# One x slab by plain load, two more by DMA transposes of their own, and W1's first slab in halves: the start of a one-core gated mix kernel

## The chip, the cores and the metric

The program runs on one core of a Trainium2 chip. The metric is device time of one execution in microseconds (us). Quoted times are medians over the runs of a kernel, and a ratio is the mean time of one kernel's runs over that of the other's runs of the same rounds on the same chip, so it is not quite the ratio of the quoted medians. A profile is one single execution; its span is about 1.3 us shorter than the time of that run.

Words used below: a *slab* is one of five 128-row pieces of the contraction dimension (D = 640), of W1 or of x. PE is the matmul engine, SP the engine that issues most DMAs, ACT and DVE the two elementwise engines. "Landing" is the moment the last of a DMA's 16 completion counts arrives.

## The reference, cut to what matters

```python
x = A_x                                        # [1, 2048, 640], bf16
g = sigmoid((x * gate_w).sum(-1))
a = ssm(x)                                     # B projection, complex scan, C projection, skip
b = gelu(x @ w1 + b1) @ w2 + b2                # w1 [640, 1728], w2 [1728, 640]
return g * a + (1 - g) * b
```

The kernel works in four quarters of 512 rows of x. Its first real work is `x @ w1` for quarter 0 and the first 1024 columns of w1: eight output tiles, five slabs each, 40 steps of 128x128 by 512 columns. This is called the first W1 group.

## The kernel before: the parts that matter

The tensor engine needs x transposed (contraction on partitions). x's slabs 0 and 1 of quarter 0 come by a plain load and are transposed on PE, with a copy from PSUM by DVE; slabs 2, and 3 with 4, come by DMA transposes. SP issues these loads one after the other, in this order:

```python
KN = 2
load("xna", "sp", ..., xn[0][:, :, 0:KN * 128], x2[0:512, 0:KN * 128]...)   # x slabs 0, 1
w1load(0, "sp", 1)                       # W1 slab 0, 256 KB
w1load(1, "sp", 1.3)
xtrans(0, range(KN, KN + 1), 1.6, 0.8)   # x slab 2, DMA transpose
w1load(2, "sp", 2)
xtrans(0, range(KN + 1, KD), 3, 1.3)     # x slabs 3 and 4, one DMA transpose
w1load(3, "sp", 4)
w1load(4, "sp", 5)
# ... then the rest of W1, the transposes of B, more of x, W2, C
```

PE runs warm-up matmuls on a constant until x arrives, then the transposes, then the first W1 group slab by slab:

```python
def f_warm():
    for n in (512,) * 6 + (256,):
        nc.tensor.matmul(PS[4][:, 0:n], one..., one..., start=True, stop=True)

for i, (k, c0, c1) in enumerate(((0, 0, 2), (0, 2, 4), (1, 0, 2), (1, 2, 4))):
    # two 128x128 transposes on PE, then a copy by DVE into xT[0][:, k, ...]
# ... (cut)
steps = [(0, 0, 0), (0, 1, 0), (0, 0, 1), (0, 1, 1)] + [(k, jf, None) for k, jf in seq if k or jf > 1]
# each step waits for its W1 slab and its x slab; slab-major order, 8 PSUM banks
```

Tile 7 of slab 0 is put off until just before tile 7 of slab 1, because its bank is used for the transposes. So PE needs slab 1 after seven steps, and 33 steps are then still to come; 24 from slab 2 on, 16 from slab 3 on, 8 from slab 4 on.

## Time and profile before

| | before |
|---|---|
| median on record at the prediction | 213.72 us (3 runs) |
| median, 6 runs beside the change | 213.16 us (212.76 to 213.74) |
| span of the profile | 211.5 us (its run took 212.76) |
| first W1 matmul | 4.57 us |
| end of the first W1 group | 13.27 us |

The profile page's chain that ended last, of the kernel before:

```profile
PE 98%; issue 0%; DVE 0%
```

The wait view for PE, same kernel (engine, line, what it waited for: us in total, times, longest):

```profile
PE ps L400 <- PEq L968: 0.8, 1, 0.8
PE ps L685 <- issue: 0.2, 1, 0.2
```

PE is the bottleneck and, in this view, waits only 0.2 us once it has begun. The timeline of PE, same kernel, cut at 3 us so that only the last three warm-up matmuls show (start us, length us, engine, line, what, count):

```profile
2.44 1.27 PE L400 MATMUL ps<-const-bfloat16-1.0 128*128 128x512 bf16 x3
3.67 1.06 PE L412 MATMUL ps<-ident,xn 128*128 128x128 bf16 x8
4.57 2.54 PE L622 MATMUL ps<-xT,W1sb 128*128 128x256 bf16 x13
6.95 0.22 PE L431 MATMUL ps<-ident,rows 128*128 128x128 bf16 x1
7.01 6.42 PE L622 MATMUL ps<-xT,W1sb 128*128 128x512 bf16 x28
13.27 1.03 PE L642 MATMUL ps<-xT,W1sb 128*128 128x512 bf16 x4
```

Start to start, a warm-up matmul of 512 columns takes 0.427 us and a W1 matmul of 512 columns 0.2157 us: PE is at half rate until about 4.5 us. (The row of the page that shows the granted clock is full throughout; it does not show this half rate.)

The timeline of SP, same kernel (start us is the moment of issue, the second number how long SP was busy issuing):

```profile
0.74 0.45 SPq L326 DMA_DIRECT2D xn<-in_A_x_dram  x1
1.25 0.96 SPq L326 DMA_DIRECT2D W1sb<-in_B_w_dram  x2
2.26 1.20 SPq L333 DMA_TRANSPOSE xT<-in_A_x_dram  x1
3.51 0.59 SPq L326 DMA_DIRECT2D W1sb<-in_B_w_dram  x1
4.15 1.28 SPq L333 DMA_TRANSPOSE xT<-in_A_x_dram  x1
5.47 2.10 SPq L326 DMA_DIRECT2D W1sb<-in_B_w_dram  x4
```

A transpose costs SP 1.20 us for one slab and 1.28 for two; a plain load 0.42 to 0.59. The DMA view of the first 7 us, same kernel (q1 is SP's queue, with packets, MB and the share of the 16 DMA engines' time that its packets took; in the lines of loads the last number is the median us from issue to landing):

```profile
DMA packets 2047, 1.30 MB, mean 186 GB/s; under 512 B 1151, under 2 KB 1663, under 8 KB 2047
...
q1 hardware_dynamic: 1959, 1.30, 69.6%
...
W1sb<-in_B_w_dram SPq DMA_DIRECT2D x5, 256.0 KB, 3.9
...
xT<-in_A_x_dram SPq DMA_TRANSPOSE x2, 4.1
```

### The profile page before, as it was taken

The page shows a single profiled execution, that of the slowest core. Times are in us where ns is not written, and L with a number is a line of the kernel's source. Part 1 is how long each engine was busy: PE and PEld are TensorE (multiplying, and loading weights), DVE is VectorE, ACT ScalarE, POOL GpSimd, SP SyncE. Part 2 cuts the span into 40 slices and gives each one's busy share as a digit, 9 for nine tenths or more (in the row PEclk, how much of TensorE's full clock was granted, in tenths as well). Part 3 has the DMA queues.
Part 4 walks back from the last instruction along what each step waited for, and adds up shares of the span by engine and source line. Part 5 has one row for each costly group of instructions (what it writes and reads, how often), then busy time and mean ns, then how long its engine had stood idle before and what let it go on. Part 6 is the DMA issues. An engine that isn't in the chain of part 4 may idle for free.

```text
span 211.5 us, 3140 instructions
## 1 busy us (share of the span) xinstructions
PE 208.1 (98%) x1266; PEld 121.2 (57%) x1276; DVE 189.3 (90%) x264; ACT 111.3 (53%) x201; POOL 3.0 (1%) x11
## 2 busy tenths in 40 slices
PE   8999999999999999999999999999999999999996
PEld 4444444444567776444466777544446777767775
DVE  2599999999999999999999969899999999899444
ACT  2588556678904334556953333456792444723330
POOL 2000000000000010000000001000000000000000
PEclk9999999999999999999999999999999999999999
DMA  5999699999100013100000014100000000010011
GB/s 164 290 246 183 158 225 300 303 213 197 42 0 3 31 38 120 62 0 0 0 3 0 0 48 143 39 23 3 0 0 2 3 31 31 31 34 0 31 34 62
DMA packets 31350, 16.35 MB, mean 77 GB/s; under 512 B 23144, under 2 KB 30440, under 8 KB 31336
## 3 DMA queue, kind: packets, MB, share of 16 engines
q1 hardware_dynamic: 30960, 14.83, 28.5%
q0 software_dynamic: 320, 1.31, 2.0%
q8 instruction: 10, 0.16, 0.3%
q14 instruction: 4, 0.03, 0.1%
q10 hardware_dynamic: 56, 0.01, 0.0%
HBM read 7.63 MB, written 2.62 MB: 48 GB/s over the span
## 4 chain that ended last, share of the span: by engine, by line
PE 98%; issue 0%; DVE 0%
PE ps L772 27%; PE ps L642 22%; PE ps L821 21%; PE ps L685 20%; PE ps L622 4%; PE ps L400 1%; PE ps L786 1%; PE ps L663 1%; PE ps L412 0%; DVE osb L855 0%; PE ps L431 0%
## 5 line engine op out<-in xcount | busy, mean ns | idle before, releaser
L772 PE MATMUL ps<-W2sb,Gl 128*128 128x320 bf16 x416 | 59.2, 299 | 0.0
L772 PEld LDWEIGHTS ps<-W2sb,Gl 128*128 128x128 bf16 x416 | 40.4, 98 | 17.1 <-issue 1.1
L642 PE MATMUL ps<-xT,W1sb 128*128 128x512 bf16 x215 | 47.5, 379 | 0.3
L821 PE MATMUL ps<-CT,H 128*128 128x320 bf16 (+2 forms) x330 | 45.5, 295 | 0.0
L725 DVE TENSOR_TENSOR_SCAN W<-atab,V 128x1280 bf16<-128x1280 f32 x16 | 44.3, 2811 | 0.3
L685 PE MATMUL ps<-xT,BT 128*128 128x512 bf16 x196 | 43.1, 379 | 0.3 <-issue 0.2
L821 PEld LDWEIGHTS ps<-CT,H 128*128 128x128 bf16 x330 | 31.9, 98 | 11.7
L800 ACT ACTIVATE E<-ps,g1col 128x320 bf16<-128x320 f32 x32 | 16.3, 526 | 39.7 <-PE ps L772 25.6
L642 PEld LDWEIGHTS ps<-xT,W1sb 128*128 128x128 bf16 x220 | 21.5, 98 | 26.0
L649 ACT ACTIVATE Gl<-ps,cols 128x512 bf16<-128x512 f32 x44 | 29.6, 688 | 10.0 <-PE ps L642 10.0
L685 PEld LDWEIGHTS ps<-xT,BT 128*128 128x128 bf16 x200 | 19.4, 98 | 23.5 <-ACT Gt L671 0.4
L694 ACT ACTIVATE U<-ps 128x512 bf16<-128x512 f32 x40 | 23.8, 597 | 15.0 <-PE ps L685 14.9
L832 ACT ACTIVATE E<-ps,gcol 128x320 bf16<-128x320 f32 x30 | 15.8, 527 | 22.6 <-PE ps L821 22.6
L759 ACT ACTIVATE ps<-b2b 128x320 f32<-128x320 bf16 x32 | 14.1, 441 | 1.1
L481 DVE TENSOR_TENSOR osb<-xg,E 128x640 bf16<-128x640 bf16 x15 | 7.3, 487 | 7.9 <-ACT E L832 7.6
L842 DVE SCALAR_TENSOR_TENSOR xg<-xn,gcol,dsk 128x640 bf16<-128x640 bf16 x16 | 13.9, 882 | 0.4
L597 DVE SCALAR_TENSOR_TENSOR scr<-xn,gwb 128x640 bf16<-128x640 bf16 x16 | 13.2, 822 | 0.4
L481 DVE TENSOR_TENSOR H<-H,V 128x1280 bf16<-128x1280 bf16 x16 | 12.5, 821 | 0.3
L481 DVE TENSOR_TENSOR V<-V,W 128x1280 bf16<-128x1280 bf16 x16 | 12.5, 821 | 0.3
L481 DVE TENSOR_TENSOR V<-mr,U 128x2560 bf16<-128x2560 bf16 x8 | 11.9, 1488 | 0.2
L481 DVE TENSOR_TENSOR H<-c,W 128x2560 bf16<-128x2560 bf16 x8 | 11.9, 1488 | 0.2
L481 DVE TENSOR_TENSOR W<-mi,U 128x2560 bf16<-128x2560 bf16 x8 | 11.9, 1483 | 0.0
(80 smaller groups left out, 99.9 us busy)
## 6 DMA issues: line engine op xcount, KB each, us to landing
out_dram<-osb SPq DMA_DIRECT2D x15, 160.0 KB, 1.8
W2sb<-in_B_w_dram SPq DMA_DIRECT2D x1, 2080.0 KB, 8.9
W1sb<-in_B_w_dram SPq DMA_DIRECT2D x5, 256.0 KB, 3.9
xn<-in_A_x_dram POOLq DMA_DIRECT2D x2, 640.0 KB, 4.6
xn<-in_A_x_dram SPq DMA_DIRECT2D x1, 640.0 KB, 7.9
W1sb<-in_B_w_dram SPq DMA_DIRECT2D x1, 480.0 KB, 5.8
W1sb<-in_B_w_dram SPq DMA_DIRECT2D x1, 400.0 KB, 6.5
xn<-in_A_x_dram SPq DMA_DIRECT2D x1, 384.0 KB, 6.0
```

Source lines behind the costliest of these rows:

```text
L481: return inc("dve", nc.vector.tensor_tensor(out=o, in0=a, in1=b, op=o_))
L642: t = nc.tensor.matmul(PS[bank][:, :], W1sb[:, k, jf * 128:(jf + 1) * 128], xT[q][:, k, :], start=(k == 0), stop=(k == KD - 1))
L649: return inc("act", nc.scalar.activation(Gl[q % 2][:, jf, :], PS[bank][:, :], ACT.Gelu_apprx_tanh, bias=b1col[:, jf:jf + 1]))
L685: t = nc.tensor.matmul(PS[bank][:, :], BT[:, ci, kd, k * 128:(k + 1) * 128], xT[q][:, kd, :], start=(kd == 0), stop=(kd == KD - 1))
L694: return inc("act", nc.scalar.activation(dst, src, ACT.Copy, scale=1.0 if ci == 0 else -1.0))
L725: t = inc("dve", nc.vector.tensor_tensor_scan(out=g[:, ci, :], data0=a, data1=v[:, ci, :], initial=0.0, op0=ALU.mult, op1=ALU.add))
L759: return inc("act", nc.scalar.activation(PS[bank][:, 0:HALF], b2b[:, cols], ACT.Copy))
L772: t = nc.tensor.matmul(PS[bank][:, 0:HALF], Gl[q % 2][:, jf, t4 * 128:(t4 + 1) * 128], W2sb[:, jf, cols], start=False, stop=False, skip_gr ...
L800: return inc("act", nc.scalar.activation(E1[c % NE][:, cols], PS[bank][:, 0:HALF], ACT.Copy, scale=g1col[:, c:c + 1]))
L821: t = nc.tensor.matmul(PS[bank][:, 0:n], H[b % NHB][:, ci, k, s * 128:(s + 1) * 128], CT[:, ci, k, cols], start=(i == 0), stop=(i == 2 * K ...
L832: return inc("act", nc.scalar.activation(E2[c % NE][:, cols], PS[bank][:, 0:HALF], ACT.Copy, scale=gcol[:, c:c + 1]))
L842: return inc("dve", nc.vector.scalar_tensor_tensor(out=xg[c % 2][:, :], in0=xn[q % 2][:, c % 4, :], scalar=gcol[:, c:c + 1], in1=dsk[:, :] ...
```

## The change

Its intent: start PE earlier. Only slab 0 of x comes by plain load, so that four PE transposes, two DVE copies and one warm-up matmul fall away. Slabs 1 and 2 each get a DMA transpose of their own, ahead of the W1 slab that goes with them. W1's slab 0 comes in halves, so that the first half is there sooner. A small filler matmul keeps PE busy while DVE copies. The diff, cut to its core:

```diff
-        KN = 2
+        KN = 1
         load("xna", "sp", ...)
-        w1load(0, "sp", 1)
+        for h in range(2):
+            f0, f1 = h * FW // 2, (h + 1) * FW // 2
+            load(f"w1_0{h}", "sp", f"l_w10{h}", W1sb[:, 0, f0:f1], B_w1[0:128, f0:f1], [("w1", 0, h)], prio=1 + 0.1 * h, lat=2.6)
+        xtrans(0, range(KN, KN + 1), 1.2, 0.8)
         w1load(1, "sp", 1.3)
-        xtrans(0, range(KN, KN + 1), 1.6, 0.8)
+        xtrans(0, range(KN + 1, KN + 2), 1.6, 0.8)
         w1load(2, "sp", 2)
-        xtrans(0, range(KN + 1, KD), 3, 1.3)
+        xtrans(0, range(KN + 2, KD), 3, 1.3)
         w1load(3, "sp", 4)
 ...
-            for n in (512,) * 6 + (256,):
+            for n in (512,) * 5 + (256,):
 ...
-        for i, (k, c0, c1) in enumerate(((0, 0, 2), (0, 2, 4), (1, 0, 2), (1, 2, 4))):
-            bank = (7, 6, 5, 7)[i]
+        for i, (k, c0, c1) in enumerate(((0, 0, 2), (0, 2, 4))):
+            bank = 7 - i
 ...
+        def f_fill():
+            return inc("pe", nc.tensor.matmul(PS[4][:, 0:192], one..., one..., start=True, stop=True))
+        op("fill", "pe", 0.2, (), [("bank", 4)], f_fill, prio=-980)
 ... (the waits of slab 0's matmuls go by half; cut)
```

More of the change, by code (lines that the diff above doesn't have):

```diff
@@ L413, in f_xt @@
                 return inc("pe", t)
-            op(f"xt{i}", "pe", 0.11 * (c1 - c0), ["xna", "ident"], [("bank", bank)], f_xt, prio=(-990, -989, -988, 2.5)[i])
+            op(f"xt{i}", "pe", 0.11 * (c1 - c0), ["xna", "ident"], [("bank", bank)], f_xt, prio=-990 + i)
             def f_xc(k=k, pt=pt, c0=c0, c1=c1):
@@ L420, in bass_gated_mix__ssm_conv_s5__dense_activation_gelu__prompt_kernel @@
             op(f"xc{i}", "dve", 0.42, [("bank", bank)], [("xT", 0, k, c0)], f_xc, prio=-2000 + i)
+        def f_fill():
+            return inc("pe", nc.tensor.matmul(PS[4][:, 0:192], one.broadcast_to([128, 128]), one.broadcast_to([128, 192]), start=True, stop=True))
+        op("fill", "pe", 0.2, (), [("bank", 4)], f_fill, prio=-980)
         XK0 = [[("xT", 0, k)] for k in range(KD)]
         XK0[0] = [("xT", 0, 0, 0), ("xT", 0, 0, 2)]
-        XK0[1] = [("xT", 0, 1, 0), ("xT", 0, 1, 2)]
         XT = {q: [("xT", q, k) for k in range(KD)] for q in range(1, NQ)}
@@ L623, in f_mm @@
                                                       start=(k == 0 and t0 == 0), stop=(k == KD - 1), skip_group_check=jf < 2))
-                op(f"m1_0_{jf}_{k}_{t0}", "pe", d_mm(t1 - t0), (XK0[k] if h is None else XK0[k][h:h + 1]) + [("w1", k)], [("bank", jf)],
+                op(f"m1_0_{jf}_{k}_{t0}", "pe", d_mm(t1 - t0), (XK0[k] if h is None else XK0[k][h:h + 1]) + ([("w1", k)] if k else [("w1", 0, jf // (NW // 2))]), [("bank", jf)],
                    f_mm, prio=pe_prio())
@@ L644, in f_mm @@
                     return inc("pe", t)
-                op(f"m1_{q}_{jf}", "pe", KD * d_mm(512), XT[q] + ([("w1", k) for k in range(KD)] if jf < NW else [("w1", "r", int(jf * 128 >= FM))]), [("bank", bank)], f_mm, prio=pe_prio())
+                op(f"m1_{q}_{jf}", "pe", KD * d_mm(512), XT[q] + ([("w1", k) for k in range(1, KD)] + [("w1", 0, 0), ("w1", 0, 1)] if jf < NW else [("w1", "r", int(jf * 128 >= FM))]), [("bank", bank)], f_mm, prio=pe_prio())
                 def f_ge(jf=jf, bank=bank):
```

## The prediction

> **What bounds it now.** The chain of waits is PE for 98% of the 211.5 us span; the wait view gives PE 0.8 us before its first matmul and 0.2 us elsewhere. The back-to-back part of the kernel cannot shrink by this change: it does the same matmuls. Only the start matters: when the first real matmul (W1 times x, quarter 0) begins, and whether slabs of W1 and x land fast enough for the 40 slab matmuls that follow.
>
> Timeline of before: 7 warm-up matmuls 0.78 to 3.5 (512 columns every 0.427 us); 8 PE transposes 3.67 to 4.57, the first released by the landing of x's 256 KB load (issued 0.74, landed 2.9 us later); first W1 matmul 4.57; from then 512 columns every 0.2155 us with no gap over 0.05 us until 13.27. So slab 1 is wanted at 6.09, slab 2 at 8.09, slab 3 at 9.81, slab 4 at 11.54. Landings (issue plus time to landing, DMA view): W1 slab 0 4.3, slab 1 5.7, x slab 2 6.3, W1 slab 2 7.2, x slabs 3-4 8.3, W1 slab 3 9.45, slab 4 10.2, first rest of W1 12.3 (wanted 13.27). Slab 3 has only 0.36 us to spare.
>
> **What the change saves.** One warm-up matmul (0.43), four PE transposes (4 x 0.107) and two copies leave; a 192-column filler (about 0.16) comes. The x load is halved in bytes, not in packets (512 of 256 B instead of 512 B; in the trace they take 18 against 27 ns): I estimate it lands 0.2 us earlier. Transposes at about 3.45, first copy 3.8 to 4.1 (0.29 us), first W1 matmul about 4.15 with the first half slab landed by then: 0.3 to 0.5 us gained, all on the critical path.
>
> **What it costs.** SP issues serially. A transpose costs it 1.20 us (one slab) or 1.28 (two), a plain load 0.42 to 0.59. The new queue has one more transpose ahead of W1's slab 1, so that slab is issued at 3.5 instead of 1.8, slab 2 at 5.5 instead of 3.5, slab 3 at about 7.4 instead of 5.5, slab 4 at 8.0 instead of 6.1. In before, loads land 3.0 to 4.1 us after issue. The queue ahead is shorter now, so I estimate about 3.1 to 3.5: slab 1 at 6.6 (wanted about 5.7), slab 2 at 8.5 to 8.9 (wanted 8.6 after the first stall), slab 3 at 10.6 to 11.0 (wanted 10.3), slab 4 in time. PE stalls of about 0.8 + 0.2 + 0.5 us replace the 0.4 gained. The first W1 group ends near 14.3 instead of 13.27. The rest shifts: the B transposes come about 1.2 us later, but have 1.5 us to spare.
>
> The Trainium skill, "TensorE: Matmul & The Clock Gate", Part 1, says half rate lasts until about 3.4 us of sustained activity, in a free-running window. This trace agrees: 0.427 us per 512 columns before, 0.2155 from 4.57. The new gaps are under 1 us, so I expect no long return to half rate; the switch may come a little late.
>
> **Prediction.** 213.72 - 0.4 + 1.1 = 214.4 us, range 213.2 to 215.5. Faster by over 2%: 0.01; within 2%: 0.97; slower by over 2%: 0.02.
>
> **What would show it.** First W1 matmul near 4.15 (right start); PE waits named after W1 or x landings before slab 1 and slab 3, about 0.5 us each or more (right cost); slab 1 issued at 3.5 and slab 3 at 7.4; everything after 20 us shifted rigidly by the same amount.
>
> **What would make it wrong.** Landing within 2.8 us of issue on the shorter queue: then the stalls nearly vanish and the result is 213.3 to 213.6. A clock switch one window late: up to 1.5 us more. The new order of DVE (gates against combines) making PE wait later on.

## The result, and the profile after

| | before | after |
|---|---|---|
| median of 6 runs | 213.16 us (212.76 to 213.74) | 214.34 us (214.09 to 214.83) |
| ratio | | 1.0055, 95% interval 1.0032 to 1.0077 |
| span of the profile | 211.5 us | 213.2 us (its run took 214.49) |
| first W1 matmul | 4.57 us | 3.94 us |
| end of the first W1 group | 13.27 us | 14.98 us |
| profile's end minus that | 198.2 us | 198.2 us |

The change is 0.55% slower, within the 2% that count as the same. PE starts its real work 0.63 us earlier and ends the first W1 group 1.71 us later; from there on both profiles take the same 198.2 us (211.5 - 13.27 and 213.2 - 14.98). So all of the loss is in the first 15 us. (Profile to profile it is 1.7 us, median to median 1.2: the profile of before fell on its fastest execution.)

The page's chain, of the changed kernel:

```profile
PE 94%; SPq 3%; DMA 2%; issue 0%; DVE 0%
```

The wait view for PE, changed kernel:

```profile
PE ps L629 <- DMA W1sb<-in_B_w_dram: 1.2, 2, 0.8
PE ps L403 <- PEq L975: 0.8, 1, 0.8
```

Two waits for W1 are new. The timeline of PE, changed kernel:

```profile
2.44 0.84 PE L403 MATMUL ps<-const-bfloat16-1.0 128*128 128x512 bf16 x2
3.13 0.61 PE L415 MATMUL ps<-ident,xn 128*128 128x128 bf16 x4
3.54 0.37 PE L426 MATMUL ps<-const-bfloat16-1.0 128*128 128x192 bf16 x1
3.94 2.38 PE L629 MATMUL ps<-xT,W1sb 128*128 128x256 bf16 x9
6.16 0.22 PE L438 MATMUL ps<-ident,rows 128*128 128x128 bf16 x1
6.83 3.94 PE L629 MATMUL ps<-xT,W1sb 128*128 128x512 bf16 x17 [0.45 <-DMA W1sb<-in_B_w_dram]
11.53 3.61 PE L629 MATMUL ps<-xT,W1sb 128*128 128x512 bf16 x16 [0.76 <-DMA W1sb<-in_B_w_dram]
```

From start to start of its matmuls, PE loses 0.62 us before slab 1, 0.11 before slab 2 and 0.93 before slab 3 (the view counts idle time only from the modelled end of the last matmul, so it says 0.45 and 0.76). And the nine matmuls of slab 0 take 2.2 us (3.94 to 6.16) instead of 1.5: in this execution the half rate lasts until about 5.4 us. PE is ready for slab 1 at 6.21 us, in before at 6.09: the whole head start of 0.63 us was gone before the first wait.

The timeline of SP, changed kernel, lines as above:

```profile
...
2.26 1.20 SPq L333 DMA_TRANSPOSE xT<-in_A_x_dram  x1
3.51 0.57 SPq L326 DMA_DIRECT2D W1sb<-in_B_w_dram  x1
4.13 1.13 SPq L333 DMA_TRANSPOSE xT<-in_A_x_dram  x1
5.31 0.58 SPq L326 DMA_DIRECT2D W1sb<-in_B_w_dram  x1
5.94 1.26 SPq L333 DMA_TRANSPOSE xT<-in_A_x_dram  x1
7.24 2.10 SPq L326 DMA_DIRECT2D W1sb<-in_B_w_dram  x4
```

Slab 1 of W1 is now issued at 3.51 (before: 1.79), slab 2 at 5.31 (3.51), slab 3 at 7.24 (5.47). The DMA view of the first 7 us, changed kernel:

```profile
DMA packets 2162, 0.98 MB, mean 140 GB/s; under 512 B 1752, under 2 KB 2008, under 8 KB 2162
...
q1 hardware_dynamic: 2074, 0.97, 68.3%
...
W1sb<-in_B_w_dram SPq DMA_DIRECT2D x2, 256.0 KB, 3.3
...
xT<-in_A_x_dram SPq DMA_TRANSPOSE x3, 3.1
```

Each transfer lands sooner after its issue (3.1 to 3.3 us instead of 3.9 to 4.1), yet fewer bytes have moved in the same 7 us: 0.98 MB instead of 1.30. That fits a queue that SP fills too slowly, but this view alone does not show it: the packets of SP's queue took almost the same share of the engines' time, 68.3% against 69.6%. Packets lasted longer, too: in the packet records of these 7 us, W1's 2 KB packets took 168 ns in the mean instead of 107 (median 84 in both). The count of bytes under the table of experiments tells more. The chain of waits in order of time, changed kernel (start us, us, what), shows what PE waited for in the end:

```profile
...
5.94 1.26 SPq L333
7.19 0.04 issue
7.24 4.16 DMA W1sb<-in_B_w_dram
11.40 0.14 issue
11.53 3.61 PE ps L629 x16
...
```

The chain no longer runs over PE in the first 11 us: it runs over SP's issues, from 0.74 us on, to W1's slab 3, which lands at 11.4 us.

A simple bound makes the profiles comparable: PE cannot end the first W1 group before a slab's landing plus its remaining steps at 0.2157 us. Landings here are issue plus time to landing, from the trace. For slab 3 this is 9.45 + 16 x 0.2157 = 12.90 in before (PE's own pace decides, 13.27) and 11.40 + 3.45 = 14.85 in the change (it ended at 14.98, with 0.14 us from landing to the first matmul).

### The profile page after: what moved, and what is told of

Its sections match the earlier page's. It is cut to its first block, busy times and chain, and to the rows that moved or that the text cites. A ratio compares the mean times of both kernels' runs of the same rounds, so it can differ in the third digit from the quotient of the medians.

```text
span 213.2 us, 3142 instructions
## 1 busy us (share of the span) xinstructions
PE 209.2 (98%) x1272; PEld 121.0 (57%) x1272; DVE 188.8 (89%) x262; ACT 111.4 (52%) x201; POOL 3.0 (1%) x11
## 4 chain that ended last, share of the span: by engine, by line
PE 94%; SPq 3%; DMA 2%; issue 0%; DVE 0%
PE ps L779 27%; PE ps L649 22%; PE ps L828 20%; PE ps L692 20%; DMA W1sb<-in_B_w_dram 2%; PE ps L629 2%; SPq L333 2%; PE ps L793 1%; SPq L326 1%; PE ps L670 1%; DVE osb L862 0%
## 5 line engine op out<-in xcount | busy, mean ns | idle before, releaser
L649 PE MATMUL ps<-xT,W1sb 128*128 128x512 bf16 x220 | 48.1, 379 | 0.0
L692 PE MATMUL ps<-xT,BT 128*128 128x512 bf16 x200 | 43.8, 379 | 0.0
L488 DVE TENSOR_TENSOR V<-mr,U 128x2560 bf16<-128x2560 bf16 x8 | 11.9, 1490 | 0.3
L488 DVE TENSOR_TENSOR H<-c,W 128x2560 bf16<-128x2560 bf16 x8 | 11.9, 1488 | 0.1
L488 DVE TENSOR_TENSOR V<-s,W 128x2560 bf16<-128x2560 bf16 x8 | 11.9, 1484 | 0.0
```

The costliest lines, as they stand in the source:

```text
L488: return inc("dve", nc.vector.tensor_tensor(out=o, in0=a, in1=b, op=o_))
L649: t = nc.tensor.matmul(PS[bank][:, :], W1sb[:, k, jf * 128:(jf + 1) * 128], xT[q][:, k, :], start=(k == 0), stop=(k == KD - 1))
L692: t = nc.tensor.matmul(PS[bank][:, :], BT[:, ci, kd, k * 128:(k + 1) * 128], xT[q][:, kd, :], start=(kd == 0), stop=(kd == KD - 1))
```

## The experiments

Theory A: SP issues serially, so each added issue holds back the W1 slabs behind it. Rival B: the transposes' many small packets slow the DMA path itself. Rival D: the changeovers between plain and transposed traffic do. Theory C: the clock; starting earlier does not pay while PE is at half rate, in one version (C1) by the chance of a free-running window, in the other (C2) because a gap in the warm-up puts off the switch. All twelve runs gave correct results.

| run | median us | before beside it | ratio (95%) | first W1 | W1 slab 3 issued, landed | end of first W1 group |
|---|---|---|---|---|---|---|
| before (profile) | 213.16 | | | 4.57 | 5.47, 9.45 | 13.27 |
| the change (profile) | 214.34 | 213.16 | 1.0055 (1.0032-1.0077) | 3.94 | 7.24, 11.40 | 14.98 |
| e1_act | 216.32 | 212.95 | 1.0139 (1.0117-1.0160) | 3.97 | 3.58, 10.86 | 16.30 |
| e2_whole | 213.81 | 212.95 | 1.0042 (1.0027-1.0057) | 4.39 | 6.78, 10.39 | 14.05 |
| e3_halves | 213.52 | 212.95 | 1.0025 (1.0013-1.0037) | 4.69 | 6.05, 10.05 | 13.70 |
| e4_pair | 213.91 | 212.95 | 1.0041 (1.0028-1.0054) | 3.95 | 6.00, 10.19 | 14.49 |
| e5_split | 213.24 | 213.20 | 1.0000 (0.9982-1.0018) | 4.68 | 6.61, 9.70 | 13.52 |
| e8_swap | 213.14 | 213.20 | 1.0002 (0.9983-1.0021) | 4.60 | 5.36, 9.05 | 13.46 |
| e6_combo | 213.21 | 213.20 | 1.0009 (0.9982-1.0037) | 4.24 | 5.53, 9.44 | 13.78 |
| e7_warm5 | 213.63 | 213.20 | 1.0025 (1.0001-1.0049) | 4.68 | 5.45, 9.18 | 13.98 |
| f1_act0 | 214.77 | 212.96 | 1.0085 (1.0059-1.0112) | 4.98 | 6.32, 10.52 | 15.14 |
| f3_combo_act0 | 215.16 | 212.96 | 1.0090 (1.0067-1.0113) | 4.88 | 5.30, 10.17 | 15.18 |
| f5_combo_act0_warm6 | 213.43 | 212.96 | 1.0024 (0.9996-1.0052) | 5.06 | 5.37, 8.95 | 15.45 |
| f2_warm5b | 214.25 | 212.96 | 1.0037 (1.0003-1.0071) | 4.79 | 5.43, 9.31 | 15.97 |

The last three columns are from one profiled execution each, so they scatter; the medians and ratios are from 5 or 6 runs. In all profiles but one, span minus the last column is 198.2 us; in e5_split it is 198.5.

Two things about all the profiles were not reported with the single runs. The first is how many bytes the DMA queues moved in the first 11 us (the DMA view of each run). With as many issues on SP as in before it is 2.52 to 2.63 MB (before, e6_combo, e7_warm5, e8_swap, f2_warm5b); with one load fewer on SP 2.65 and 2.66 (f3_combo_act0, f5_combo_act0_warm6); with one load more 2.31 and 2.35 (e3_halves, e4_pair); with one transpose more 2.21 and 2.22 (e5_split, e2_whole), or 2.24 if a load fewer goes with it (f1_act0); with a load and a transpose more, which is the change, 2.04; in e1_act 1.82. In this order the bytes fall as SP's issue time grows. The second is that W1's slab 3 landed 3.6 to 4.2 us after its issue in eleven of the 14 profiles, although the issue lay anywhere from 5.36 to 7.24 us; the other three are e5_split (3.09), f3_combo_act0 (4.87) and e1_act (7.28). But one landing in one profile is not exact: f3_combo_act0 and f5_combo_act0_warm6 have the same loads and issued slab 3 within 0.1 us of each other, and it landed at 10.17 and 8.95.

### e1_act: W1's slabs 1 to 4 issued by ACT

```diff
-        w1load(1, "sp", 1.3)      # and 2, 3, 4, between the transposes
+        for k in range(1, KD):    # after ACT's four small loads
+            w1load(k, "act", k)
```

> The changed kernel, but W1's slabs 1 to 4 are issued by ACT (after its four small loads) and not by SP between the transposes. Same bytes, same packets, same transposes. Theory A (SP issues serially, so every added transpose holds back the W1 slab behind it): slabs 1 to 4 are issued between about 2.5 and 4.5 us instead of 3.5 to 8.3, PE's waits before slab 1 (0.67 us) and slab 3 (0.93 us) shrink to under 0.3 us in sum, first W1 group ends near 13.4 us instead of 14.98, time 212.9 to 213.4, level with the kernel before. Rival B (the transposes' small packets slow the DMA path itself): waits of 1 us or more stay, time 214 or more. Theory C (clock): whatever the loads do, slab 0's nine matmuls still take until about 6.1 us because the clock is at half rate until about 5.3.

The issue times came out as theory A said, the rest did not: 216.32 us, the slowest of all (214.97 to 218.88). ACT issued slabs 1 to 4 between 2.56 and 4.24 us, but they landed at 8.0, 9.3, 10.9 and 11.5; x's slab 1, issued at 2.27 as in the change, landed at 8.2 instead of 5.3, and even the second half of W1's slab 0, issued by SP at 1.80 as in the change, at 6.2 instead of 4.7. The wait view for PE of this run:

```profile
PE ps L627 <- DMA xT<-in_A_x_dram: 1.5, 2, 0.8
PE ps L627 <- DMA W1sb<-in_B_w_dram: 1.3, 1, 1.3
...
```

With plain loads on one issuing engine's queue and transposes on the other's, both in flight, all of them got slow. In the packet records, 105 packets of 2 KB took over 150 ns before 11 us, against 60 in the change (median 85 and 84 ns). So early issue alone did not buy early landing here. By the numbers forecast for it (waits of 1 us or more, 214 us or more) rival B fits this run; why the mixture is so slow is not settled by it. PE began at 3.97 us, much as in the change; but here it was at full rate already (matmuls of 256 columns 0.109 us apart), against theory C's 5.3 us.

### e2_whole: the change with W1's slab 0 in one load

```diff
-        for h in range(2):
-            load(f"w1_0{h}", "sp", ...)     # two halves
+        load("w1_00", "sp", "l_w100", W1sb[:, 0, 0:FW], B_w1[0:128, 0:FW], [("w1", 0, 0), ("w1", 0, 1)], prio=1, lat=2.6)
```

> The changed kernel with W1's slab 0 in one load again: one SP issue of about 0.45 to 0.54 us less ahead of everything. Theory A: slabs 1 to 4 are issued and land about 0.45 us earlier, the wait before slab 3 falls from 0.93 to about 0.4 to 0.5, the one before slab 1 from 0.67 to 0.2 to 0.4; time about 213.8 (0.5 less than the change). Rival: the halves are what lets PE start early, without them the first W1 matmul moves from 3.94 to over 4.3 and the time is the same or worse.

The time came out as expected, 213.81 us. All later issues moved forward by 0.46 us, slab 3 landed at 10.39 instead of 11.40, and PE waited for none of slabs 1 to 4; that is more than the theory asked for. The first W1 matmul moved back to 4.39, and the halves' earlier start was not missed. What was left over, in this profile, was the clock: PE stayed at half rate until about 6.4 us. And measured against the before of the same rounds the gain is smaller than the medians say: ratio 1.0042 instead of 1.0055, 0.3 us, with overlapping intervals, so that no gain at all is not excluded.

### e3_halves: before with only W1's slab 0 in halves

```diff
-        w1load(0, "sp", 1)
+        for h in range(2):
+            load(f"w1_0{h}", "sp", ...)     # as in the change
```

> The kernel before with only W1's slab 0 in halves. Theory A: one SP issue more, slabs 1 to 4 land about 0.5 us later; they had 0.36 us to spare at slabs 1 and 3, so PE waits about 0.1 to 0.3 us in all: time 213.2 to 213.5, within 0.15% of before. If the halves alone were the cost of the change, it would be 214 or more; if they help, first W1 matmul before 4.57 and time under 213.

Dearer than expected: 213.52 us, 0.57 above the before beside it, where 0.1 to 0.3 was forecast. One more issue of 0.47 us near the head of the queue moved slab 3's landing by 0.60 us (9.45 to 10.05) and slab 4's from 10.2 to 11.9 (two other looks at the loads of before, e7_warm5 and f2_warm5b, have slab 4 at 11.1 and 11.0). The bound from slab 4 is 11.90 + 8 x 0.2157 = 13.63; the group ended at 13.70. PE shows no wait in this profile, because its clock switched late (about 5.3 us) and the slabs came just in time; but with these landings it could not have ended before 13.63, 0.36 after the profile of before. So the loss of 0.57 us in the medians fits an early issue that is paid for nearly one for one; that the landings, and not the clock, caused it is argued from the bound and not seen as a wait.

### e4_pair: the change with x's slabs 1 and 2 in one transpose

```diff
-        xtrans(0, range(KN, KN + 1), 1.2, 0.8)
+        xtrans(0, range(KN, KN + 2), 1.2, 1.3)
         w1load(1, "sp", 1.3)
-        xtrans(0, range(KN + 1, KN + 2), 1.6, 0.8)
```

> The changed kernel with x's slabs 1 and 2 in one transpose ahead of W1's slab 1. A two-slab transpose costs SP about 1.28 us, two single ones 2.3 to 2.4. Same transposed bytes, even earlier. Theory A: W1's slabs 2, 3 and 4 are issued about 1.1 us earlier, the wait before slab 3 (0.93 us) vanishes; the wait before slab 1 may grow by 0.2 to 0.5 us because 128 KB more lie ahead of it; time about 213.6 to 213.9. Rival B (transposed bytes slow the path): no gain, 214.3 or more.

As theory A expected, the wait before slab 3 is gone (issued 1.24 us earlier, landed 1.20 earlier), and the bound moved to slab 1, which lands at 7.45 instead of 6.70 because both x slabs now go ahead of it: 7.45 + 32 x 0.2157 = 14.35 (one postponed tile of slab 0 had already run); the group ended at 14.49. The time was the 213.91 us forecast, but against its own before that is a gain of only 0.3 us on the change (1.0041 against 1.0055), again with overlapping intervals. Rival B in its first form, that the transposed bytes themselves set the time, falls: the same bytes, transposed even earlier, did not cost more.

### e5_split: before with x's slabs 3 and 4 in two single transposes

```diff
-        xtrans(0, range(KN + 1, KD), 3, 1.3)
+        xtrans(0, range(KN + 1, KN + 2), 3, 0.8)
+        xtrans(0, range(KN + 2, KD), 3.5, 0.8)
```

> The kernel before with only one thing changed: x's slabs 3 and 4 come by two single transposes back to back instead of one of two slabs. Same bytes, same packets in the same order, same number of changes between plain and transposed traffic, same PE start. Theory A (serial issue on SP): W1's slab 3 is issued at about 6.6 instead of 5.47 us and lands at about 10.4 to 10.6 instead of 9.45; PE wants it at 9.8 and waits 0.5 to 0.8 us; time 0.5 to 0.8 above before, 213.5 to 213.8. Theory D (what costs is each changeover between plain and transposed packets in the DMA engines, not SP's issue): slab 3 lands as before, no wait, time within 0.15 of before.

Theory A fails here as it was put. The timeline of SP, this run, shows the added issue time (two transposes 2.43 us, where one took 1.28):

```profile
...
4.13 2.43 SPq L333 DMA_TRANSPOSE xT<-in_A_x_dram  x2
6.61 1.53 SPq L326 DMA_DIRECT2D W1sb<-in_B_w_dram  x3
```

Slab 3 was issued 1.14 us later and landed only 0.25 later, at 9.70; PE did not wait for it, and the time stayed level (ratio 1.0000). This looks like theory D, but there is another reading. It is argued from the latencies and not seen directly. In before, transfers from W1's slab 1 on land 3.7 to 4.1 us after issue, in the change x's slab 1, W1's slab 1 and x's slab 2 land after 3.1 to 3.2: so I read about 0.9 us of before's latency as a queue of earlier transfers. Late issue time behind such a backlog would be hidden from the next slab; early issue time, before a backlog exists, would not. Call this A2. The late issue time was not free, though: 2.21 MB moved in the first 11 us instead of 2.55, with the same bytes to move and the same changeovers as in before, which theory D does not explain; slab 4 landed 0.5 us later and both loads of the rest of W1 about 1.2 us later (12.32 to 13.47, 13.54 to 14.72). PE had slack for most of it. In this profile the transpose of B landed 2 us later than in before (19.1 instead of 17.1) and PE lost about 0.3 us there, and 0.1 at the rest of W1; the median does not show it.

### e8_swap: before with W1's slab 2 ahead of x's slab 2

```diff
-        w1load(2, "sp", 2)       # was issued after the transpose of x slab 2
+        w1load(2, "sp", 1.5)
```

> The kernel before with W1's slab 2 issued ahead of x's slab 2: same issues, same SP time up to slab 3, but the two transposes now follow each other, so there are two changes between plain and transposed traffic instead of four. Theory D: slab 3 (issued at 5.47 as before) lands 0.3 to 0.5 us earlier than 9.45, and fewer 2048 B packets take over 0.15 us (53 before). Theory A alone: slab 3 lands at 9.45 within 0.15. Time level with before in either case (212.8 to 213.2), since PE has no wait to lose there.

Level with before, as both theories said. Slab 3 landed at 9.05, 3.7 us after its issue. That is 0.40 earlier than in the profile of before, but two other looks at the same load order (e7_warm5, f2_warm5b) have it at 9.18 and 9.31, and 0.11 of it is the earlier issue, so what fewer changeovers save there is somewhere from 0 to 0.3 us. Slow packets of 2 KB did fall, from 53 to 29. Theory D is at most a small part, and not settled beyond that.

### e6_combo: the change's start with before's number of issues

```diff
-        (W1 slab 0 in two halves)
+        (W1 slab 0 in one load)
-        xtrans(0, range(KN, KN + 1), 1.2, 0.8)
-        w1load(1, "sp", 1.3)
-        xtrans(0, range(KN + 1, KN + 2), 1.6, 0.8)
+        w1load(1, "sp", 1.1)
+        xtrans(0, range(KN, KN + 2), 1.3, 1.3)
```

> The changed kernel's start (one x slab by plain load, four PE transposes, five and a half warm-up matmuls), but W1's slab 0 whole, slab 1 next, then x's slabs 1 and 2 in one transpose: as many SP issues as before, slabs 2 and 3 issued at about 3.6 and 5.5 as before. Theory A: no PE wait over 0.2 us for W1 or x, first W1 matmul 4.3 to 4.4, time 212.5 to 213.0, 0 to 0.4 below before: it should beat the change by about 1.2. If the single-slab start itself costs (cold clock, gaps), it stays at 213.5 or more.

213.21 us: it beats the change by about 1.0 us (1.0009 against 1.0055 of before; the intervals overlap only from 1.0032 to 1.0037), but it does not beat before. Slab 3 was issued at 5.53 and landed at 9.44, just as in before. The early start (4.24 us) bought nothing: PE was at half rate until about 5.1 us, and then lost 0.45 us after slab 0, where a copy by DVE and x's slabs 1 and 2 (landed at 6.51) came within 0.1 us of each other.

### e7_warm5 and f2_warm5b: before with five and a half warm-up matmuls, twice

```diff
-            for n in (512,) * 6 + (256,):
+            for n in (512,) * 5 + (256,):
```

> The kernel before with five and a half instead of six and a half warm-up matmuls: PE idles from about 3.1 to 3.67 us. Theory C1 (the switch to full rate falls anywhere, by the phase of a free-running window): time within 0.2 of before, switch anywhere from 4 to 7 us. Theory C2 (a gap in the warm-up puts the switch off; in the change and in two variants it came at 5.3, 6.2 and 5.9 us, in before near 4.5): switch after 5 us and time 0.3 to 0.8 above before.

> The same kernel as the one before with five and a half warm-up matmuls, again, for a second sample of time and of the switch to full rate: C2 expects a ratio of 1.001 to 1.004 again and a switch after 5 us; C1 expects a ratio within 0.1% of 1 and a switch anywhere from 4 to 7 us.

The same source in two groups of runs. Both were slower, by 0.25% and 0.37%, and both intervals narrowly exclude no difference: C2's forecast. (One warm-up matmul less makes the gap and also shortens the activity before it; the runs do not part the two.) The timelines of PE, first e7_warm5:

```profile
...
3.71 1.17 PE L412 MATMUL ps<-ident,xn 128*128 128x128 bf16 x8 [0.43 <-DMA xn<-in_A_x_dram]
4.68 3.15 PE L622 MATMUL ps<-xT,W1sb 128*128 128x256 bf16 x13
```

then f2_warm5b:

```profile
...
3.83 1.17 PE L412 MATMUL ps<-ident,xn 128*128 128x128 bf16 x8 [0.55 <-DMA xn<-in_A_x_dram]
4.79 4.90 PE L622 MATMUL ps<-xT,W1sb 128*128 128x256 bf16 x13
```

The same 13 matmuls of slab 0 and 1 that take 2.54 us in before take 3.15 and 4.90: the switch to full rate came at about 5.9 and 9.8 us. The runs of these two scatter from 213.0 to 215.5 us, those of before from 212.7 to 214.1. So chance is still at work (C1 is right that the moment varies by several us between executions of one kernel), but a gap seems to shift the odds.

Over all 14 profiles: where PE had no gap over 0.3 us between warm-up and first W1 matmul, the switch came at 4.0, 4.2, 4.5, 4.5, 5.3, 5.4 and 6.0 us (e1_act, e5_split, before, e8_swap, e3_halves, the change, e4_pair); with a gap of 0.57 to 1.12 us, at 5.1, 5.9, 6.4, 8.0, 8.2, 8.5 and 9.8 us (e6_combo, e7_warm5, e2_whole, f1_act0, f3_combo_act0, f5_combo_act0_warm6, f2_warm5b). A gap is counted here from the start of the last matmul plus its columns at half rate, so it is larger than the idle time in the views. Most of these kernels differ in other ways too, one profile stands for each, and e6_combo had a gap and was level with before: this is a tendency, not a shown cause.

### f1_act0: the change with W1's slab 0, whole, issued by ACT first of all

```diff
-        for h in range(2):
-            load(f"w1_0{h}", "sp", ...)
+        load("w1_00", "act", "l_w100", W1sb[:, 0, 0:FW], B_w1[0:128, 0:FW], [("w1", 0, 0), ("w1", 0, 1)], prio=1, lat=2.6)
```

> The changed kernel with W1's slab 0 in one load that ACT issues first of all, so that SP's queue of transposes and W1 loads starts about 1.0 us earlier than in the change (0.5 earlier than with slab 0 whole on SP). All three transposes and all six changeovers stay. Theory A2 (SP's issue time starves the DMA path early, before a backlog has built up, and then counts one for one; late issue time behind a backlog is absorbed, as x's slabs 3 and 4 in two transposes showed): W1's slab 2 lands at about 7.7 to 8.0 instead of 8.74, slab 3 at 9.6 to 10.3 instead of 11.39, PE waits 0.6 us or less in sum, time 213.0 to 213.6. Theory D (changeovers): slab 3 still after 10.8, time 213.9 or more.

The landings moved nearly as A2 said, both just past its ranges and short of theory D's 10.8: slab 2 at 8.09 (forecast 7.7 to 8.0), slab 3 at 10.52 (9.6 to 10.3; the change 11.40), and PE waited for no slab afterwards. The time did not: 214.77 us. The wait view for PE of this run shows what took its place:

```profile
PE ps L413 <- DMA xn<-in_A_x_dram: 0.9, 1, 0.9
PE ps L401 <- PEq L973: 0.8, 1, 0.8
```

W1's slab 0 now ran ahead of x's first load, which landed at 4.15 instead of 3.09. PE idled for 0.9 us, began at 4.98, and stayed at half rate until about 8 us. The experiment supports by its landings that SP's early issue time counts, and says nothing by its time, because it brought a second effect with it that I had not foreseen.

### f3_combo_act0 and f5_combo_act0_warm6: the combination with slab 0 on ACT

```diff
-        load("w1_00", "sp", ...)
+        load("w1_00", "act", ...)          # f3 and f5
-            for n in (512,) * 5 + (256,):
+            for n in (512,) * 6 + (256,):  # f5 only
```

> The combined version (one x slab by plain load, slab 0 whole, slab 1, then x slabs 1 and 2 in one transpose) with W1's slab 0 issued by ACT: everything behind it about 0.5 us earlier on SP. Theory A2: x's slabs 1 and 2 land at about 6.0 instead of 6.5, the 0.45 us wait before W1's slab 1 vanishes, time 212.7 to 213.1, 0.1 to 0.5 below before.

> The version just named with six and a half warm-up matmuls, so that PE is busy without a gap until the transposes; first W1 matmul at about 4.3 to 4.4. If gaps in the warm-up put off the switch to full rate (C2), the switch comes before 5 us and the time is 0.1 to 0.4 below the version with five and a half. If the phase is chance (C1), the two agree within 0.2.

Both missed for the same reason as f1_act0: x's first load landed at 4.05 and 4.24, so PE idled 0.8 and 0.6 us and began at 4.88 and 5.06. The medians are 215.16 and 213.43 us; the longer warm-up is better by more than the 0.1 to 0.4 forecast (ratios 1.0090 and 1.0024), although in the one profiled execution of each the switch came late (8.2 and 8.5 us). The profiled execution of f5_combo_act0_warm6 was its slowest, 214.95 us against 213.23 to 213.89 for the other five, so its profile does not stand for its median. Neither beats before. No version tried does.

## Why the prediction was right, point by point

The time was predicted as 214.4 with a range of 213.2 to 215.5, and was 214.34: inside, and within 2% as forecast. The mechanism was right: SP's added issue time makes W1's slabs land late, and PE's waits for them outweigh the earlier start. Several sizes were not right, the sum was added up wrongly, and the errors partly cancelled.

- **"0.3 to 0.5 us gained, all on the critical path."** The first W1 matmul came at 3.94, earlier than the 4.15 forecast: 0.63 us ahead. But it was not all on the critical path, in fact none of it was: slab 0 ran mostly at half rate and took 0.70 us longer, and PE stood ready for slab 1 at 6.21 instead of 6.09. Even at full rate PE would only have waited longer, since slab 1 landed at 6.70.
- **"The switch may come a little late."** It was named, and the sum holds no term for it. It took 0.70 us of slab 0 in the profile.
- **The issue times** (slab 1 at 3.5, slab 2 at 5.5, slab 3 at about 7.4) were 3.51, 5.31 and 7.24. The landings forecast at 6.6, 8.5 to 8.9 and 10.6 to 11.0 were 6.7, 8.7 and 11.4.
- **"PE stalls of about 0.8 + 0.2 + 0.5 us."** They were 0.62, 0.11 and 0.93. The last term was mis-sized: I took 3.1 to 3.5 us from issue to landing on a shorter queue; that held for slabs 1 and 2 (3.2 and 3.4), but slab 3 took 4.2, perhaps because a queue had formed again.
- **The sum.** It was added up wrongly. Stalls of 0.8 + 0.2 + 0.5 us less the 0.4 gained are the 1.1 of the last line, and the first W1 group was to end near 14.3 instead of 13.27; the last line then takes off the same 0.4 a second time. So the terms say +1.1 over before and the last line +0.7. Measured: +1.2 by medians, +1.7 between the two profiles: 0.70 (half rate) + 0.06 (a small transpose that now runs before slab 1) + 0.62 + 0.11 + 0.93 - 0.63 = 1.79, less 0.06 for the same transpose in before. That 214.4 lies so close to 214.34 is luck: the 0.4 taken off twice nearly makes up for a start from 213.72, the median of the first three runs, where the kernel before ran at 213.16 beside the change. The terms themselves, +1.1, fit the medians; against the two profiles they miss by 0.6, about what the half rate took.
- **"Everything after 20 us shifted rigidly"** held: 198.2 us from the end of the group in both profiles. B's transposes did not stall PE, and the new order of work on DVE cost nothing.
- **The cause.** That SP's issue time is the cost was tested. Giving the changed start as many issues as before had (e6_combo) brought the landing of slab 3 back to 9.44 us and the time level with before. Taking part of the issue time out (e2_whole 0.46 us, e4_pair 1.24 us) removed the waits before slab 3, but brought only some 0.3 us each, less than the intervals can tell apart, and in the profiles a late clock switch or the landing of slab 1 took over as the bound. Adding 0.47 us to before at the head of the queue (e3_halves) cost 0.53 us by the ratio. Over all variants with one exception (e1_act) the bytes moved in 11 us fall with each issue added on SP, also in e5_split, which keeps before's bytes and changeovers. But as a rule for the time it is too simple: 1.14 us added late (e5_split) cost nothing that the median shows, since slab 3 landed only 0.25 us later and PE had slack for what landed later still. The prediction's own arithmetic, issue time plus a latency of 3.1 to 3.5 us, leaves out that the latency itself moves: from 3.2 us for slab 1 to 4.2 for slabs 3 and 4 in the change alone.

What stays open: why plain loads and transposes from two issuing queues slow each other so much (e1_act); how large the cost of a changeover is within one queue (0 to 0.3 us by e8_swap); why W1's packets lasted longer in the change (168 ns in the mean against 107), while their medians agree; whether a backlog is what hid the late issue time in e5_split; and what exactly decides the moment of the switch to full rate.

The Trainium skill helped and misled in turn. "TensorE: Matmul & The Clock Gate", Part 1, describes a half-rate start and a free-running window of activity, and warns not to fit a specific count of slow matmuls; the traces agree on the half rate (0.427 against 0.2157 us for 512 columns) and on a moment that varies (5.9 and 9.8 us in two profiles of the same source). That the window is free-running no run here shows. "DMA: Bandwidth & Descriptors", section "Issuing engines are not separate DMA queues", says that spreading issues over engines saves only the sequencer's time, "which is usually small relative to the DMA itself". Here that time was on the chain that ended last, 1.1 to 1.3 us for each transpose of 128 or 256 KB against 3.1 to 3.9 us from its issue to its landing in the change; and saving it by a second engine (e1_act, f1_act0) was a loss for other reasons.

## What to carry to other kernels

At the start of a kernel, look at the issuing engine's timeline before the consumer's. Here each issue added on SP cost bytes moved in the first 11 us, and it cost time where PE had no slack for the slabs behind it; where PE had slack (e5_split) it cost none that could be measured. An earlier first matmul was worth nothing here, because the landing of the next operands set the end and PE was still at half rate. And be careful with a gap in a warm-up to gain a few tenths of a us: the two groups of runs with such a gap in before reached 214.8 and 215.5 us, where no run of before took more than 214.1.

## What the Trainium skill lacked or had wrong

- "TensorE: Matmul & The Clock Gate", Part 1, speaks of gaps of more than about 3.4 us as what throttles PE. It gives no figure for a shorter gap within the warm-up. Here a gap of 0.57 to 1.12 us went with a later switch to full rate: 5.1 to 9.8 us in seven profiles, against 4.0 to 6.0 us in seven without a gap over 0.3 us; before with one warm-up matmul less was 0.25% and 0.37% slower in its two groups of runs.
- "DMA: Bandwidth & Descriptors", section "Issuing engines are not separate DMA queues", calls the sequencer's time usually small. Here SP spent 1.13 to 1.28 us (in before and in the change) on each transpose of one or two slabs, 0.42 to 0.59 us on a plain load, and slab 3, issued 1.77 us later in the change, landed 1.95 us later.
- The same section says that DMAs of different issuing engines interleave on the same engines. It lacks that plain loads from one engine beside transposes from another can be very slow: x's slab 1 took 5.9 us from issue to landing (3.1 when both came from SP), and the run was 1.39% slower than before (the change 0.55%).
- "Advanced Engine Details and Errata", section "X-Bar Transpose (TRN2)", says transpose DMAs are as fast as regular ones. From issue to landing the runs do not contradict it: 256 KB of x took 3.9 and 4.1 us transposed, 256 KB of W1 3.0 to 4.2 us plain (in the change and in before; bandwidth was not measured). The section lacks the issue time, which differed: 1.26 and 1.28 us against 0.42 to 0.59.
- "TensorE: Matmul & The Clock Gate", Part 1, cautions in general that trace events of the clock can be unreliable. It lacks that the granted clock in the profile can read 1.00 all through the half-rate start, as it did here where 512 columns took 0.427 us instead of 0.2157, so that the half rate must be read from the spacing of matmuls.
